# Two reads of the attention output in a fused kernel: 32-column TensorE tiles for one, split float32r products for part of the other

## The chip, the core and the metric

The kernel runs on one core of one Trainium2 chip. The metric is the device time of one execution in microseconds (us). The engines are named as in the profile: PE is TensorE's matmul side, PEld its weight loads, DVE is VectorE, ACT is ScalarE, POOL is GpSimd and SP is SyncE, which issues nearly all DMAs.

## What is computed

An attention between 2048 tokens and 128 state rows, followed by two feed-forward blocks, all in float32. Cut to what matters here:

```python
# x: (B=4, H=8, S=512, D=64)    state: (4, 8, 32, 64)
a      = softmax(x @ state^T / 8);   xread = a  @ state    # tokens read the state
a2     = softmax(state @ x^T / 8);   sread = a2 @ x        # the state reads the tokens
t = concat([xread, sread], axis=2) -> (2176 tokens, 512)   # 544 per batch
t = ((t @ w_a) * (t @ w_b)) @ w_out                        # d_ff 1536
t = softplus(t @ w_in) @ w_out2                            # d_ff 2048
```

The 128 rows of `sread` (32 states in 4 batches) go through the feed-forward blocks as tokens of their own.

## The kernel before

Every operation is written down first as a step with a cost for each engine that could do it (`Plan.add`). `Plan.go` then runs through the steps as a list scheduler: an engine that is free takes, among the steps that are ready by the costs, the one that was written first, and the order found in this way is the order of each engine's instruction queue. A step that writes a new buffer also needs a free slot in its space (`Plan.place`, line 172), and the buffers of some helpers ask that a number of slots stay free (`spare`). F is the space of 44 float32 slots, R that of 50 float32r slots (128 x 512 words each; ten of them are set aside for the last batch), and K is the eight PSUM banks. When the x of a batch is no longer needed, its four slots join R (`xr` in the trace; for the last batch F, `xf`).

Products take one of two forms. `Products.one` with float32 operands is one product, which the trace shows as two MATMUL records. `Products.three` with operands split into a high and a low float32r half is three products, one record each. `split_to` (line 500) makes the halves: a cast to float32r (`copy`, line 422, on ACT or DVE) and a subtraction (`tt`, line 430, on DVE, or on POOL where DVE has a queue). Every matmul of `one` has line 476 in the trace, every transpose line 491. `convert` (line 524) turns the loaded 64-bit weights into float32 (ACT line 415, DVE lines 438, 442 and 430).

The first feed-forward block is done in NHS = 6 parts `s` of 256 gate columns, and in each part over the four batches `b`. Part 0 also holds the attention: `scores_of`, `state_softmax`, and `sread(b)` (line 677), which takes the softmax of the state's scores and multiplies it with x. In `sread` a bank `pr[g]` holds four of the eight heads. For each of the four chunks `c` of 128 tokens and each pair of heads `j`, one product has 64 weight columns (two heads of 32 states) and 128 moving columns (the two heads' 64 columns of x). Of its 64 x 128 result only the two blocks of a head with itself are used. ACT then scales the 128 x 128 block by the softmax sums, PE turns it, and four copies of 64 x 64 put the used blocks into `srt`.

`state_w` multiplies the state with the weights of a part, `gates_of(s, b)` gives the gates of the tokens of batch `b`, `y_part` multiplies them with `w_out`. `read_x(s)` (line 792) gives the gates of the 128 `sread` tokens: four float32 products of 128 x 128 weights from `srt` with 512 columns of `ab[s, p]` (the converted `w_a` and `w_b`). For parts 0 and 1 it is written in part 1, from part 2 on right after `gates_of(s, 0)`; `read_y(s)` uses the result. The second block follows, in which `split_y` splits the result of a batch and `bring_w2` brings and splits the weights `w_in` and `w_out2`; its first three units are brought in part 5.

Of the kernel before, what the change touches and what calls it, by code (L numbers as in the profile page):

```python
# [12 lines left out]
AF = mybir.ActivationFunctionType  # L13
# [4 lines left out]
P = 128  # L18
# [99 lines left out]
def made(x):  # L118
    return x.ap() if isinstance(x, Ref) else x
# [209 lines left out]
def attention_moe_moe2(ctx, tc, x, state, w_a, w_b, w_out, w_in, w_out2, out):  # L329
# [12 lines left out]
    B, H, S, D = x.shape  # L342
# [5 lines left out]
    KD = DM // P  # L348
# [4 lines left out]
    scale = 1.0 / float(D) ** 0.5  # L353
# [21 lines left out]
    def small():  # L375

        return Buf(M, 1)

    def cols(ap):

        out = ap
        if isinstance(ap, Ref):
            b, was = ap.buf, ap.buf.at
            if was is None:
                b.at = b.space.tiles[0][0]
            if b.space in X:
                b.space.tiles[0][3].setdefault("tile", None)
            out = shaped(ap)
            b.at = was
        n = 1  # L390
        for k in out[1:]:
            n *= k
        return n
# [8 lines left out]
    def in_psum(*aps):  # L402
        return any(isinstance(a, Ref) and a.buf.space is K for a in aps)


    def act_us(n, psum=False):
        return 0.165 + (0.00086 if psum else 0.0009) * n
# [4 lines left out]
    def activation(o, i, func, **kw):  # L412
        also = [v for v in kw.values() if isinstance(v, Ref)]
        acc = [kw["accum_out"]] if "accum_out" in kw else []
        give = lambda: nc.scalar.activation(  # L415
            made(o), made(i), func, **{k: made(v) for k, v in kw.items()})
        plan.add({"act": (act_us(cols(o), in_psum(i)), give)}, [i, *also], [o, *acc])

    def copy(o, i):
        n, ps = cols(o), in_psum(i)  # L420
        ways = {
            "act": (act_us(n, ps), lambda: nc.scalar.copy(made(o), made(i))),  # L422
            "dve": (dve_us(n, ps), lambda: nc.vector.tensor_copy(made(o), made(i)),  # L423
                    *([] if ps else [True])),
        }
        plan.add(ways, [i], [o])

    def tt(o, a, b, op):
        n, ps = cols(o), in_psum(a, b)
        put = lambda eng: lambda: eng.tensor_tensor(  # L430
            out=made(o), in0=made(a), in1=made(b), op=op)
        ways = {"dve": (dve_us(n, True), put(nc.vector), *([] if ps else [True]))}
        if not ps:
            ways["pool"] = (0.23 + 0.00215 * n, put(nc.gpsimd))
        plan.add(ways, [a, b], [o])

    def ts(o, i, s1, op0):
        give = lambda: nc.vector.tensor_scalar(made(o), made(i), s1, None, op0=op0)  # L438
        plan.add({"dve": (dve_us(cols(o), False), give, True)}, [i], [o])
# [7 lines left out]
    def reduce(o, i, op):  # L447
        give = lambda: nc.vector.tensor_reduce(  # L448
            out=made(o), in_=made(i), axis=AX.X, op=op)
        plan.add({"dve": (dve_us(cols(i), True), give)}, [i], [o])  # L450

    def reciprocal(o):
        plan.add({"dve": (0.2, lambda: nc.vector.reciprocal(made(o), made(o)))}, [o], [o])  # L453
# [46 lines left out]
    def split_to(i, hi, lo):  # L500
        copy(hi, i)
        tt(lo, i, hi.bitcast(F32), ALU.subtract)

    def split(v, spare=0):

        h, l = Buf(R, v.run, spare), Buf(R, v.run, spare)
        split_to(v.all(), h.all(), l.all())
        return h, l
# [96 lines left out]
    def xn(b, p, c):  # L605

        return xs[b][p].rearrange("q (h c d) -> q c h d", h=2, d=D)[:, c]
# [10 lines left out]
    for n, i in enumerate((zs, zt)):  # L618
        ps = Buf(K, 1)
        m = Products()  # L620
# [8 lines left out]
    srt = Buf(F, 1)  # L629
# [4 lines left out]
    def quarter(b, i):  # L634

        return i ^ b % 2

    def turned(src, i=0):

        ps = Buf(K, 2)  # L640
        m = Products()
        for g in range(2):
            for c in range(4):
                m.turn(ps[g][:, c * P:c * P + P], src[i + g][:, c * P:c * P + P])
        m.end()
        return ps
# [30 lines left out]
    def sread(b):  # L677
        t = raw.pop(b)
        nm, sum2 = small(), small()
        nm_, sum_ = nm[0][:, 0:2], sum2[0][:, 0:2]  # L680
        reduce(nm_, t.all(), ALU.max)
        ts(nm_, nm_, -scale, ALU.mult)
        for g in range(2):
            activation(
                t[g], t[g], AF.Exp, bias=nm[0][:, g:g + 1], scale=scale,
                accum_out=sum2[0][:, g:g + 1],
            )
        ts(sum_, sum_, 1e-9, ALU.add)
        reciprocal(sum_)
        pa = turned(t)  # L690
        a2 = Buf(F, 2)
        copy(a2.all(), pa.all())
        pr = Buf(K, 2)
        m = Products()
        for g in range(2):
            for c in range(4):
                for j in range(2):
                    m.one(
                        pr[g][64 * j:64 * j + 64, 0:P].rearrange("p (h d) -> p h d", h=2),
                        a2[g][:, c * P + 64 * j:c * P + 64 * j + 64],  # L700
                        xn(b, 2 * g + j, c), c == 0, c == 3, us=0.23,
                    )
        m.end()

        for g in range(2):
            sd = a2[g][:, 0:P]
            activation(sd, pr[g][:, 0:P], AF.Identity, scale=sum2[0][:, g:g + 1])
            m = Products()
            m.turn(pr[g][:, P:2 * P], sd)
            m.end()  # L710
        for i in range(2):
            for g in range(2):
                src = pr[g][64 * i:64 * i + 64, P:2 * P]
                src = src.rearrange("p (j q n) -> p j q n", j=2, q=2)
                if b % 2:
                    src = src[:, :, ::-1]
                copy(
                    srT[64 * i:64 * i + 64, 2 * g:2 * g + 2, NS * b:NS * b + NS], src[:, :, i]
                )
# [39 lines left out]
    sw, ab = {}, {}  # L759
# [32 lines left out]
    def read_x(s):  # L792

        ps = Buf(K, 1)
        m = Products()
        for p in range(KD):
            m.one(ps[0], srt[0][:, p * P:p * P + P], ab[s, p][p % 2], p == 0, p == KD - 1, us=0.87)
        m.end()
        t = Buf(F, 1)
        ab_ = t[0][:, 0:HW]  # L800
        copy(ab_, ps[0][:, 0:HW])
        tt(ab_, ab_, ps[0][:, HW:W], ALU.mult)
        pt = Buf(K, 1)
        m = Products()
        for j in range(2):
            m.turn(pt[0][:, j * P:j * P + P], t[0][:, j * P:j * P + P])
        m.end()
        if s == 0 and len(Y32) == B:
            gs[s] = Buf(F, 1)
            copy(gs[s][0][:, 0:HW], pt[0][:, 0:HW])  # L810
            return
        gs[s] = Buf(R, 1)
        split_to(pt[0][:, 0:HW], gs[s][0][:, 0:HW], gs[s][0][:, HW:W])

    gs, wo, y = {}, {}, {}

    def bring_wo(s):
        w = fetch(("wo", s), 2)
# [111 lines left out]
    for s, b in steps:  # L930
# [15 lines left out]
        if s == SREAD:  # L946
            sread(b)
        if s and b == 0:
            if s > SREAD + 1:
                read_x(s)  # L950
            bring_wo(s)
        if s == SREAD + 1 and b < SREAD + 2:
            read_x(b)
# [85 lines left out]
    for q, b, k in steps:  # L1039
# [5 lines left out]
        for c0, n in cuts_of(b):  # L1045
            ps = Buf(K, 1)
            m = Products()
            for p in range(KD):
                c = p * HW + ff % 2 * P
# [47 lines left out]
```

## Time and profile before

| | before |
|---|---|
| median of 3 runs | 759.64 us (759.14 to 759.84) |
| the profiled execution | 758.87 us, span 757.1 us |
| PE busy | 733.0 us (97%), 3828 records |
| DVE busy | 583.4 us (77%), 735 instructions |
| ACT busy | 401.8 us (53%), 644 instructions |
| POOL busy | 32.7 us (4%), 19 instructions |
| granted TensorE clock | 0.998 of full speed |

Times in the views count from the start of the span. A share of busy time is a mean over stages with different limits, so the stage is read first and the share second. A group of matmuls is given with its first start and the end of its last record; the ends of matmuls are modelled, so the time that a group takes on PE is better read from its start to the start of what follows.

### The profile page before, as it was taken

The page shows a single profiled execution, that of the slowest core. Times are in us where ns is not written, and L with a number is a line of the kernel's source. Part 1 is how long each engine was busy: PE and PEld are TensorE (multiplying, and loading weights), DVE is VectorE, ACT ScalarE, POOL GpSimd, SP SyncE. Part 2 cuts the span into 40 slices and gives each one's busy share as a digit, 9 for nine tenths or more (in the row PEclk, how much of TensorE's full clock was granted, in tenths as well). Part 3 has the DMA queues.
Part 4 walks back from the last instruction along what each step waited for, and adds up shares of the span by engine and source line. Part 5 has one row for each costly group of instructions (what it writes and reads, how often), then busy time and mean ns, then how long its engine had stood idle before and what let it go on. Part 6 is the DMA issues. An engine that isn't in the chain of part 4 may idle for free.

```text
span 757.1 us, 9417 instructions
## 1 busy us (share of the span) xinstructions
PE 733.0 (97%) x3828; PEld 581.8 (77%) x3828; DVE 583.4 (77%) x735; ACT 401.8 (53%) x644; POOL 32.7 (4%) x19
## 2 busy tenths in 40 slices
PE   5889999999999999999999999999999999999996
PEld 4447677777777777778888798888988889888895
DVE  4999987768677868889999767665769888665673
ACT  4767753232323424424395586656666667656562
POOL 0000000000001000000211100100110011100000
PEclk9999999999999999999999999999999999999999
DMA  9611321103112113133111000000111100001112
GB/s 309 205 59 54 130 93 54 58 1 112 56 44 68 56 56 111 56 110 114 56 56 56 1 1 1 0 1 1 55 57 56 55 1 1 1 0 56 56 56 70
DMA packets 22351, 45.17 MB, mean 60 GB/s; under 512 B 2212, under 2 KB 6308, under 8 KB 22308
## 3 DMA queue, kind: packets, MB, share of 16 engines
q1 hardware_dynamic: 21764, 43.52, 17.0%
q10 hardware_dynamic: 544, 1.05, 0.4%
q8 instruction: 30, 0.49, 0.3%
q14 instruction: 13, 0.11, 0.0%
HBM read 40.11 MB, written 4.46 MB: 59 GB/s over the span
## 4 chain that ended last, share of the span: by engine, by line
PE 77%; DVE 19%; issue 1%; DMA 1%; ACT 1%; SPq 0%; DVEq 0%
PE PS L476 76%; DVE SF L442 6%; DVE SF L430 5%; DVE SR L430 3%; DVE SM L448 2%; DVE SF L438 2%; PE PS L491 1%; DMA x<-in_x 1%; DVE xr L430 1%; ACT SF L415 0%; SPq L459 0%; DVE SM L453 0%; ACT SR L422 0%; DVE SR L423 0%; DVE xf L430 0%
## 5 line engine op out<-in xcount | busy, mean ns | idle before, releaser
L476 PE MATMUL PS<-SR 128*128 128x512 f32 (+2 forms) x1878 | 461.0, 378 | 2.5 <-DVE SF L430 1.2
L476 PEld LDWEIGHTS PS<-SR 128*128 128x128 f32 x1878 | 340.1, 188 | 71.2 <-issue 3.6
L415 ACT ACTIVATE SF<-SF 128x512 f32<-128x512 f32 (+3 forms) x259 | 165.7, 650 | 14.1 <-DMA SF<-in_moe_w_b 7.2
L476 PE MATMUL PS<-SR,xr 128*128 128x512 f32 (+2 forms) x568 | 159.3, 384 | 0.0
L430 DVE TENSOR_TENSOR SF<-SF,PS 128x1024 f32<-128x1024 f32 (+2 forms) x100 | 97.7, 985 | 47.9 <-PE PS L476 47.4
L422 ACT CAST SR<-SF 128x1024 fp32r<-128x1024 f32 (+3 forms) x103 | 75.5, 735 | 107.5 <-DVE SF L430 107.2
L442 DVE SCALAR_TENSOR_TENSOR SF<-SF 128x512 f32<-128x512 f32 (+4 forms) x139 | 131.6, 949 | 1.1
L476 PEld LDWEIGHTS PS<-SR,xr 128*128 128x128 f32 x568 | 105.0, 188 | 24.3 <-issue 2.6
L422 ACT COPY SF<-PS 128x1024 f32<-128x1024 f32 (+3 forms) x87 | 62.3, 737 | 110.2 <-PE PS L476 103.9
L476 PE MATMUL PS<-xr,SR 128*128 128x512 f32 x378 | 120.3, 392 | 0.0
L430 DVE TENSOR_TENSOR SR<-SF,SR 128x512 fp32r<-128x512 f32 (+3 forms) x96 | 82.9, 868 | 23.4 <-ACT SR L422 23.3
L442 DVE SCALAR_TENSOR_TENSOR SF<-PS,SF 128x512 f32<-128x512 f32 (+2 forms) x77 | 46.6, 605 | 54.9 <-ACT SF L415 54.9
L476 PEld LDWEIGHTS PS<-xr,SR 128*128 128x128 f32 x378 | 70.9, 188 | 16.8 <-DVE SF L430 0.8
L430 DVE TENSOR_TENSOR SF<-SF 128x512 f32<-128x512 f32 (+3 forms) x97 | 79.7, 822 | 1.7
L476 PE MATMUL PS<-SF 64*32 64x512 f32 (+2 forms) x592 | 65.2, 551 | 1.0 <-ACT SF L422 1.0
L438 DVE TENSOR_SCALAR SF<-SF 128x1024 uint32<-128x1024 uint32 x67 | 45.9, 689 | 18.8 <-ACT SF L415 18.4
L415 ACT ACTIVATE SF<-PS 128x512 f32<-128x512 f32 (+2 forms) x76 | 39.9, 526 | 30.8 <-PE PS L476 29.8
L430 POOL TENSOR_TENSOR SF<-SF 128x1024 f32<-128x1024 f32 x9 | 24.0, 2663 | 507.4 <-DVE SF L442 386.1
L476 PEld LDWEIGHTS PS<-SF 64*32 64x32 f32 (+1 forms) x592 | 22.0, 117 | 26.8 <-issue 22.6
L422 ACT CAST xr<-SF 128x1024 fp32r<-128x1024 f32 (+3 forms) x26 | 21.3, 821 | 33.9 <-DVE SF L430 33.9
L422 ACT CAST SR<-PS 128x1024 fp32r<-128x1024 f32 (+2 forms) x24 | 20.6, 866 | 20.1 <-PE PS L491 12.1
L476 PE MATMUL PS<-xr,xr 128*128 128x512 f32 x80 | 29.0, 391 | 0.0
(56 smaller groups left out, 274.1 us busy)
## 6 DMA issues: line engine op xcount, KB each, us to landing
SF<-in_moe_w_out SPq DMA_DIRECT2D x14, 1024.0 KB, 4.9
SF<-in_moe_w_in SPq DMA_DIRECT2D x8, 1024.0 KB, 5.4
SF<-in_moe_w_a SPq DMA_DIRECT2D x11, 512.0 KB, 4.1
SF<-in_moe_w_b SPq DMA_DIRECT2D x11, 512.0 KB, 5.0
x<-in_x SPq DMA_DIRECT2D x8, 512.0 KB, 9.9
out<-SF SPq DMA_DIRECT2D x13, 256.0 KB, 2.6
out<-xf SPq DMA_DIRECT2D x4, 256.0 KB, 2.6
SF<-in_moe_w_a ACTq DMA_DIRECT2D x1, 512.0 KB, 4.2
```

The costliest lines, as they stand in the source:

```text
L415: give = lambda: nc.scalar.activation(made(o), made(i), func, **{k: made(v) for k, v in kw.items()})
L422: "act": (act_us(n, ps), lambda: nc.scalar.copy(made(o), made(i))),
L430: put = lambda eng: lambda: eng.tensor_tensor(out=made(o), in0=made(a), in1=made(b), op=op)
L438: give = lambda: nc.vector.tensor_scalar(made(o), made(i), s1, None, op0=op0)
L442: give = lambda: nc.vector.scalar_tensor_tensor(out=made(o), in0=made(a), scalar=s, in1=made(b), op0=op0, op1=op1)
L448: give = lambda: nc.vector.tensor_reduce(out=made(o), in_=made(i), axis=AX.X, op=op)
L476: self.all.append(lambda: nc.tensor.matmul(made(o), made(w), made(x), start=first, stop=last, **kw))
L491: self.all.append(lambda: nc.tensor.transpose(made(o), made(i), ident))
```

## The change

`sread` computes for each head alone: 32 weight columns (32 states) and 64 moving columns (64 columns of x), on the column tile of 32 that its place in the bank names. Only the used blocks are computed, the block that is scaled and turned has 64 columns in place of 128, and the planner's cost of a product goes from 0.23 to 0.03 us, with twice as many products. `read_x` keeps the float32 products for parts 0 and 1; from part 2 on it splits `srt` (once) and the four blocks `ab[s, 0]` to `ab[s, 3]` (as two pairs), and makes three float32r products in place of each float32 product.

```diff
             for c in range(4):
-                for j in range(2):
+                for i in range(4):
+                    q = 32 * quarter(b, i)
                     m.one(
-                        pr[g][64 * j:64 * j + 64, 0:P].rearrange("p (h d) -> p h d", h=2),
-                        a2[g][:, c * P + 64 * j:c * P + 64 * j + 64],
-                        xn(b, 2 * g + j, c), c == 0, c == 3, us=0.23,
+                        pr[g][q:q + 32, 0:D], a2[g][:, c * P + q:c * P + q + 32],
+                        xn(b, 2 * g + i // 2, c)[:, i % 2], c == 0, c == 3, us=0.03,
+                        tile_position=(0, q),
                     )
...
-            sd = a2[g][:, 0:P]
-            activation(sd, pr[g][:, 0:P], AF.Identity, scale=sum2[0][:, g:g + 1])
+            sd = a2[g][:, 0:D]
+            activation(sd, pr[g][:, 0:D], AF.Identity, scale=sum2[0][:, g:g + 1])
             m = Products()
-            m.turn(pr[g][:, P:2 * P], sd)
+            m.turn(pr[g][0:D, P:2 * P], sd)
...
-                src = pr[g][64 * i:64 * i + 64, P:2 * P]
-                src = src.rearrange("p (j q n) -> p j q n", j=2, q=2)
+                src = pr[g][0:D, P:2 * P].rearrange("p (j q n) -> p j q n", j=2, q=2)
...
     def read_x(s):
         ps = Buf(K, 1)
+        whole = s < WHOLE
+        if not whole:
+            if not srparts:
+                srparts.append(split(srt))
+            whl = split(ab[s, 0], 6) + split(ab[s, 2], 6)
         m = Products()
         for p in range(KD):
-            m.one(ps[0], srt[0][:, p * P:p * P + P], ab[s, p][p % 2], p == 0, p == KD - 1, us=0.87)
+            c = slice(p * P, p * P + P)
+            w = [ab[s, p]] if whole else whl[p // 2 * 2:p // 2 * 2 + 2]
+            m.three(ps[0], [i[0][:, c] for i in ([srt] if whole else srparts[0])],
+                    [i[p % 2] for i in w], p == 0, p == KD - 1)
...
-    gs, wo, y = {}, {}, {}
+    WHOLE = 2
+    gs, wo, y, srparts = {}, {}, {}, []
```

## Rows read from the trace of the kernel before

**Rows 1.** The page: busy us, share, instructions; then the granted PE clock by slices.

```profile
PE 733.0 (97%) x3828; PEld 581.8 (77%) x3828; DVE 583.4 (77%) x735; ACT 401.8 (53%) x644; POOL 32.7 (4%) x19
...
PEclk9999999999999999999999999999999999999999
```

**Rows 2.** Busy us by stretch (columns as in the first line).

```profile
core 0: us, PE busy (x) PEld busy (x) DVE busy (x) ACT busy (x) POOL busy (x), PEclk, DMA share, GB/s
...
40.00:60.00 20.00, 17.41 (x141) 10.56 (x140) 19.93 (x25) 14.01 (x26) 0.00 (x0) 1.00 0.32 107
60.00:80.00 20.00, 19.03 (x140) 13.90 (x138) 19.93 (x26) 15.24 (x26) 0.00 (x0) 1.00 0.16 53
...
200.00:250.00 50.00, 50.00 (x255) 37.39 (x261) 36.37 (x36) 14.96 (x17) 2.39 (x1) 1.00 0.18 63
250.00:300.00 50.00, 50.00 (x248) 37.65 (x233) 38.80 (x38) 15.84 (x18) 0.00 (x0) 1.00 0.20 64
300.00:330.00 30.00, 30.00 (x161) 21.43 (x160) 25.54 (x24) 11.74 (x12) 0.00 (x0) 1.00 0.26 88
330.00:355.00 25.00, 25.00 (x112) 20.49 (x111) 21.24 (x22) 10.31 (x12) 0.00 (x0) 1.00 0.42 136
355.00:422.00 67.00, 67.00 (x299) 55.50 (x298) 66.72 (x71) 39.22 (x60) 13.79 (x5) 1.00 0.16 52
422.00:747.00 325.00, 324.62 (x1563) 277.44 (x1562) 231.07 (x370) 205.16 (x385) 15.23 (x6) 1.00 0.07 23
```

**Rows 3.** PE in order of time: start, us, group, idle before and its releaser.

```profile
49.95 1.97 PE L476 MATMUL PS<-x,SF 128*64 128x128 f32 x32
...
53.98 1.95 PE L476 MATMUL PS<-SF 64*32 64x256 f32 x48
57.11 1.66 PE L476 MATMUL PS<-SR 128*128 128x512 f32 x6 [1.18 <-DVE SF L430]
...
62.92 1.66 PE L476 MATMUL PS<-SR 128*128 128x512 f32 x6 [0.77 <-DVE SR L430]
64.52 1.97 PE L476 MATMUL PS<-x,SF 128*64 128x128 f32 x32
...
77.97 3.01 PE L476 MATMUL PS<-SR 128*128 128x512 f32 x12 [0.16 <-ACT SF L422]
80.91 1.97 PE L476 MATMUL PS<-x,SF 128*64 128x128 f32 x32
82.81 1.65 PE L476 MATMUL PS<-SR 128*128 128x512 f32 x6
85.86 1.28 PE L491 MATMUL PS<-ident,SF 128*128 128x128 f32 x10 [1.40 <-DVE SF L430]
...
96.02 1.97 PE L476 MATMUL PS<-x,SF 128*64 128x128 f32 x32
97.92 1.66 PE L476 MATMUL PS<-SR 128*128 128x512 f32 x6
```

**Rows 4.** PE groups by shape: tile, moving operand, records; busy us, mean ns of one.

```profile
L476 PE MATMUL PS<-SF 64*32 64x512 f32 x384 | 24.9, 597 | 0.1
L476 PE MATMUL PS<-x,SF 128*64 128x128 f32 x128 | 7.9, 276 | 0.0
L476 PE MATMUL PS<-SF 64*32 64x256 f32 x128 | 5.1, 385 | 1.0 <-ACT SF L422 1.0
```

**Rows 5.** PE in order of time, the first eight records of one group alone.

```profile
53.98 0.45 PE L476 MATMUL PS<-SF 64*32 64x256 f32 x8
```

**Rows 6.** PE in order of time around `read_x(2)`, and a run of float32r products.

```profile
167.41 3.59 PE L476 MATMUL PS<-SF 128*128 128x512 f32 x8
170.44 3.31 PE L476 MATMUL PS<-SR,xr 128*128 128x512 f32 x12
173.59 0.38 PE L491 MATMUL PS<-ident,SF 128*128 128x128 f32 x2
...
347.04 5.60 PE L476 MATMUL PS<-SR 128*128 128x512 f32 x24
352.48 0.39 PE L476 MATMUL PS<-xr 128*128 128x512 f32 x1
```

**Rows 7.** Groups by shape between 100 and 430 us: the two halves of a split.

```profile
L422 ACT CAST SR<-SF 128x1024 fp32r<-128x1024 f32 x25 | 26.2, 1049 | 31.3 <-DVE SF L430 31.2
L430 DVE TENSOR_TENSOR xr<-SF,SR 128x1024 fp32r<-128x1024 f32 x5 | 6.1, 1223 | 0.0
```

**Rows 8.** PE in order of time: the wait at the end of the busy DVE stretch.

```profile
422.82 7.37 PE L476 MATMUL PS<-SR 128*128 128x512 f32 x30 [0.32 <-ACT SR L422]
```

## The prediction

> **What bounds the kernel now.** I read the page first: PE is busy 97% of the span at full clock [rows 1], so PE time looks like what is for sale. A mean hides stages, so the table of stretches came next. From 40 to 80 us DVE is busy 19.93 us of every 20, while PE is not [rows 2]. In that stage PE waits for DVE again and again: 1.18 us at 57.11, 0.77 at 62.92 and 1.40 at 85.86 [rows 3]. Up to about 86 us the bound is therefore DVE. From 100 us on PE is busy all the time, while DVE has room: it is idle 13.6 us of 200 to 250, 11.2 of 250 to 300 and 4.5 of 300 to 330 [rows 2]. From 355 to 422 both are full, DVE with 66.72 of 67 us [rows 2], and at the end of it PE waits 0.32 us for a cast that hangs on DVE [rows 8]. After that PE is the bound up to the last output, with 0.4 us idle in 325 [rows 2]. So PE time removed before 86 us should be worth nothing, after 86 us its full length, provided that DVE keeps up at 422.
>
> **The state's read on 32-column tiles.** There are four `sread` groups, at 49.95, 64.52, 80.91 and 96.02 us, each of 32 records, which are 16 products of two records [rows 3]. A group lasts 1.97 us from its first start to the end of its last record; without the last record's own 0.27 us [rows 4], 1.70 us for 32 records is far less than 32 x 0.276 = 8.8 us, so records overlap. The tile is 128 x 64 [rows 4], so two products lie side by side, 16 records deep, and one step of a tile takes about 1.70 / 15 = 0.11 us. The change makes 32 products of two records, in four tiles side by side: again 16 records deep. What becomes shorter is the step. Records with 512 and 256 moving columns differ by 597 - 385 = 212 ns, 0.83 ns a column [rows 4]; 64 columns fewer than 128 take away 53 ns. The step falls from 0.11 to about 0.056 us, and the group costs PE 16 x 0.056 = 0.90 us in place of some 1.75 us: 0.85 us less.
>
> No row shows four tiles of 128 x 32, so this has bounds on both sides. On the good side, eight records on tiles of 64 x 32 run side by side: the first eight of a group take 0.45 us in all, of which one record is 0.385, so they start (0.45 - 0.385) / 7 = 9 ns apart [rows 4, 5]. At 9 ns a record 64 records would need 0.6 us, less than the 0.90 of the columns, so the columns bind. On the bad side, if the four tiles didn't overlap at all, 64 x 0.056 = 3.6 us, 1.85 us more than now. A middle row is 48 records of 64 x 32 tiles in 1.95 us [rows 3], at most 1.95 / 48 = 41 ns each with moving operands up to eight times longer. I take 0.90 because it is nearest to both rows with small tiles, in which records do overlap; the range keeps 0.90 to 3.6.
>
> The Trainium skill (TensorE: Matmul & The Clock Gate, section "Wait — 56ns, not 53.3ns?") speaks against the step: it states that the distance from one start to the next never drops below about 25 ns, however small the product is. By that an estimate for 64 records is 1.6 us, and the gain of a group would be 0.15 in place of 0.85 us. The 9 ns above don't bear it out between different tiles [rows 4, 5].
>
> What counts of it: the first three groups lie in the DVE-bound stage. If they end earlier, PE waits longer for DVE at 57.11, 62.92, 77.97 and 85.86 [rows 3], and I cost their gain at nothing. The work that hides it is DVE's; if that cover were gone, they would bring up to 3 x 0.85 = 2.55 us. The fourth group at 96.02 lies behind the last of these waits and counts in full: -0.85 us. Scaling and turning 64 columns instead of 128 saves ACT and PE some tenths in the same places, which I leave at nothing; the four copies stay as they are. No DMA is added or moved.
>
> **The gates of these tokens as float32r.** A float32 `read_x` has 8 records. From its start at 167.41 to the transposes at 173.59 lie these 8 and 12 float32r records, 6.18 us [rows 6]. A float32r record takes (352.48 - 347.04) / 24 = 0.2267 us [rows 6], so 12 are 2.72 us, and the 8 are 6.18 - 2.72 = 3.46 us. The change puts 12 float32r records in place of these 8: 2.72 us. Saved per part 0.74 us, and with four parts (2 to 5), all of them in the stretch in which PE is the bound: -2.96 us.
>
> For it, each of the four parts gets two splits of 128 x 1024, and `srt` one of 128 x 512. A split is a cast of 1.05 us on ACT and a subtraction of 1.22 us on DVE [rows 7]. In all that is some 9 casts (about 9 us) and 10.4 us of subtractions, about 2.4 us per part on DVE. DVE is idle 11 to 14 us of each 50 us there, ACT over 30 [rows 2], and the inputs (`ab`) exist a part ahead, since `state_w` of the part has read them. So I cost the splits at nothing; the cover is DVE's idle time, and without it each part would cost up to 2.4 us. Part 5 has least of it, but still 4.5 us before 330 and 3.8 us from 330 to 355 [rows 2].
>
> At 422 PE now waits 0.32 us [rows 8] for the end of a stretch in which DVE has no idle time. If PE comes there 3.8 us earlier, DVE must too. Most of its work from 330 on is released by PE's results (the sums and splits of the outputs), which come earlier by the same amount; the weights of the second block don't. I take 0.3 us as lost, the size of the wait that is there now; the bound is the whole 3.8 us.
>
> **Sum.** -0.85 - 2.96 + 0.3 = -3.5 us against the profiled execution of 758.87 us (span 757.1 us): 755.4 us. The median of the runs lies 0.77 us above that execution, so the forecast for the median is 759.64 - 3.5 = 756.1 us, with its own range of 754.9 to 757.6.
>
> **The rivals.**
> - **DVE keeps the end at 422.** PE arrives early and waits. For it: 66.72 us busy of 67 [rows 2], and the existing wait [rows 8]. Against it: 8.3 us of idle DVE time from 300 to 355 [rows 2]. If all but 1 us of the gain is given back there: 758.6 us.
> - **The order changes in the DVE-bound stage.** The planner is told that an `sread` takes 32 x 0.03 = 0.96 us instead of 16 x 0.23 = 3.68, where the trace has 1.75. Its picture of PE becomes better by over 1 us four times, and DVE's queue may come out in an order in which PE waits less. If the first three groups then count too: 756.1 - 2.6 = 753.5 us. Against it: DVE's work there stays what it is and is already back to back [rows 2].
> - **The splits come late because slots are short** (the slower side). Two splits of `ab` need 8 slots of R and `srt` two for good. By the code the start of a part holds some 39 of the 52 (8 for the softmax of two batches, 8 of `w_out` in two parts, some 14 of `state_w`, 8 gates, 1), and each split asks for 6 spare. A split that only starts when `gates_of` has freed slots puts a cast and a subtraction, 1.05 + 1.22 = 2.27 us [rows 7], in front of `read_x` or of the halves of `state_w`, which ask for slots at the same time. PE's order is fixed, so it waits. At 2.27 us per part the four parts cost 9.1 us against 3.5 gained: 765.2 us. It decides from 3.5 / 4 = 0.9 us of waiting in each part. For it: the narrow count. Against it: inputs that exist a part ahead.
> - **The small tiles don't overlap.** Each group then costs 1.85 us more: the fourth in full, the other three 5.5 us less the waits that they fill (1.18 + 0.77 + 0.16 + 1.40 = 3.5 us [rows 3]), so 2.0 us. Together 756.1 + 0.85 + 1.85 + 2.0 = 760.8 us. If records are only kept apart so that a group costs what it does now, it is 757.0 us, inside the forecast's own range.
>
> **How the numbers follow.** About what a measurement of this kernel can tell from no change is 0.2%, 1.5 us: faster is under 758.1 us, slower over 761.2. Forecast 0.47, of which 0.46 is faster and 0.01 within 0.2%. Better order 0.15, faster. DVE at 422 0.17: 0.14 within, 0.03 faster. Late splits 0.13: 0.11 slower, 0.02 within. Tiles without overlap 0.08: 0.04 within, 0.03 slower, 0.01 faster. That gives faster 0.65, same 0.21, slower 0.14. The range from 752.8 to 760.4 us takes in the forecast, the better order, DVE at 422 and the milder forms of the last two, and leaves out under 2 in 10.
>
> **What would show it.** In the changed kernel's trace: four groups of 64 records on 128 x 32 tiles, each about 0.9 us from its start to what follows, against 3.6 us without overlap; PE's waits for DVE before 88 us longer than now by about what the first three groups save; from part 2 on 12 float32r records in 2.72 us where 8 float32 records took 3.46; DVE between 100 and 330 us busier by some 2.4 us per part, with no PE wait for line 430 or 422 in these parts; at about 419 a PE wait of at most some tenths. A PE wait of over 0.9 us in each part, or one of 3 us near 419, would make the prediction wrong, and so would a first stage that ends at another time than now.

## The result: 749.6 us, a gain of 10.0 us, nearly three times the forecast

The changed kernel takes 749.64 us (median of 4 runs, 749.54 to 749.76), the kernel before 759.65 us. The ratio is 0.9868, with an interval from 0.9856 to 0.9879. The forecast was 756.1 us, and its range ended at 752.8: the sign is right, the size is not. The profiled execution took 749.62 us, its span 747.8.

The page of the changed kernel (busy us, share, instructions), to be laid beside [rows 1]:

```profile
PE 725.4 (97%) x3972; PEld 580.3 (78%) x3972; DVE 591.7 (79%) x741; ACT 405.4 (54%) x647; POOL 56.3 (8%) x28
```

PE is busy 7.6 us less, DVE 8.3 us more, and POOL has nine instructions more. The stretches of the changed kernel, with the columns of [rows 2]:

```profile
40.00:60.00 20.00, 18.59 (x175) 10.72 (x174) 19.93 (x25) 15.56 (x28) 0.00 (x0) 1.00 0.15 54
60.00:80.00 20.00, 20.00 (x251) 15.35 (x250) 19.86 (x26) 15.83 (x26) 0.00 (x0) 1.00 0.15 54
...
40.00:100.00 60.00, 58.59 (x587) 41.60 (x586) 57.33 (x70) 45.00 (x78) 0.00 (x0) 1.00 0.21 72
...
347.00:412.00 65.00, 64.98 (x289) 53.50 (x288) 61.99 (x69) 40.59 (x61) 10.93 (x4) 1.00 0.22 74
```

This is the riddle. Between 40 and 80 us DVE is as full as before (19.93 and 19.86 of 20, against 19.93 and 19.93), yet PE has hardly any gap left: 1.41 us in 20, then none, where it had 2.59 and 0.97. The forecast had said that PE's waits there would become longer.

PE of the changed kernel in order of time (start, us, group, idle before and its releaser; last, the first float32 `read_x`):

```profile
43.19 1.09 PE L491 MATMUL PS<-ident,x 128*128 128x128 f32 x8 [1.11 <-DVE SF L430]
...
50.24 1.10 PE L476 MATMUL PS<-x,SF 128*32 128x64 f32 x64
51.27 1.98 PE L476 MATMUL PS<-SF 128*128 128x512 f32 x4
...
54.43 3.03 PE L476 MATMUL PS<-SR 128*128 128x512 f32 x12
...
61.28 2.78 PE L491 MATMUL PS<-ident,SF 128*128 128x128 f32 x24
...
65.01 1.10 PE L476 MATMUL PS<-x,SF 128*32 128x64 f32 x64
66.04 1.65 PE L476 MATMUL PS<-SR 128*128 128x512 f32 x6
...
77.67 1.10 PE L476 MATMUL PS<-x,SF 128*32 128x64 f32 x64
...
90.81 1.10 PE L476 MATMUL PS<-x,SF 128*32 128x64 f32 x64
...
101.76 3.59 PE L476 MATMUL PS<-SF 128*128 128x512 f32 x8
```

The same two marks stand in the kernel before, in its order of time on PE:

```profile
42.89 1.09 PE L491 MATMUL PS<-ident,x 128*128 128x128 f32 x8 [1.11 <-DVE SF L430]
...
74.02 1.91 PE L491 MATMUL PS<-ident,SF 128*128 128x128 f32 x16
...
109.21 3.60 PE L476 MATMUL PS<-SF 128*128 128x512 f32 x8
```

From the transposes of x to the first `read_x` is therefore 109.21 - 42.89 = 66.32 us before and 101.76 - 43.19 = 58.57 after. This stretch, called the first stage below, is 7.75 us shorter. The forecast for it was 0.85. The waits of 1.18, 0.77, 0.16 and 1.40 us [rows 3] are gone; the two waits that are left, 0.30 and 1.11 us, come before 43.19, so between the two marks PE isn't idle at all.

### The profile page after: what moved, and what is told of

The parts are those of the page before. It is cut to its first block, busy times and chain, and to the rows that moved or that the text cites. A ratio compares the mean times of both kernels' runs of the same rounds, so it can differ in the third digit from the quotient of the medians.

```text
span 747.8 us, 9721 instructions
## 1 busy us (share of the span) xinstructions
PE 725.4 (97%) x3972; PEld 580.3 (78%) x3972; DVE 591.7 (79%) x741; ACT 405.4 (54%) x647; POOL 56.3 (8%) x28
## 4 chain that ended last, share of the span: by engine, by line
PE 89%; DVE 7%; ACT 1%; DMA 1%; issue 1%; DVEq 0%; ACTq 0%
PE PS L476 88%; DVE SF L430 2%; DVE SF L442 1%; PE PS L491 1%; DVE SR L430 1%; DMA SF<-in_moe_w_b 1%; ACT SF L415 1%; DVE SM L448 1%; DVE SF L438 1%; ACT SF L422 0%; ACT xr L422 0%; DVE SR L423 0%; DVE xr L430 0%; ACT SR L422 0%; DVE SM L453 0%
## 5 line engine op out<-in xcount | busy, mean ns | idle before, releaser
L476 PE MATMUL PS<-SR 128*128 128x512 f32 (+2 forms) x1986 | 513.6, 379 | 0.0
L476 PEld LDWEIGHTS PS<-SR 128*128 128x128 f32 x1986 | 362.4, 188 | 70.7 <-issue 2.9
L476 PE MATMUL PS<-SR,xr 128*128 128x512 f32 (+2 forms) x544 | 171.7, 376 | 0.2 <-DVE SR L430 0.2
L415 ACT ACTIVATE SF<-SF 128x512 f32<-128x512 f32 (+3 forms) x246 | 152.9, 631 | 12.9 <-DMA SF<-in_moe_w_b 5.7
L430 DVE TENSOR_TENSOR SF<-SF,PS 128x1024 f32<-128x1024 f32 (+2 forms) x126 | 117.2, 942 | 38.0 <-PE PS L476 37.1
L442 DVE SCALAR_TENSOR_TENSOR SF<-SF 128x512 f32<-128x512 f32 (+4 forms) x117 | 103.1, 885 | 0.5
L476 PEld LDWEIGHTS PS<-xr,SR 128*128 128x128 f32 x338 | 63.4, 188 | 18.9 <-DVE SR L430 2.3
L476 PE MATMUL PS<-SF 64*32 64x512 f32 (+2 forms) x560 | 51.5, 549 | 1.1 <-ACT SF L422 1.0
L422 ACT CAST xr<-SF 128x1024 fp32r<-128x1024 f32 (+2 forms) x26 | 23.0, 884 | 31.8 <-DVE SF L430 31.8
L491 PE MATMUL PS<-ident,SF 128*128 128x128 f32 (+1 forms) x128 | 19.2, 284 | 10.7 <-DMA SF<-in_state 8.3
```

The source lines that it names most:

```text
L415: give = lambda: nc.scalar.activation(made(o), made(i), func, **{k: made(v) for k, v in kw.items()})
L430: put = lambda eng: lambda: eng.tensor_tensor(out=made(o), in0=made(a), in1=made(b), op=op)
L442: give = lambda: nc.vector.scalar_tensor_tensor(out=made(o), in0=made(a), scalar=s, in1=made(b), op0=op0, op1=op1)
L476: self.all.append(lambda: nc.tensor.matmul(made(o), made(w), made(x), start=first, stop=last, **kw))
L491: self.all.append(lambda: nc.tensor.transpose(made(o), made(i), ident))
```

## The experiments

The first theory is that of the prediction: up to 86 us DVE sets the pace. The second is its rival "better order": the planner's cost of the `sread` products, 3.68 us in all against 1.89 in the trace [rows 3], put steps in a wrong order, and a smaller number alone removes PE's waits. "First stage" in the table is measured as above in each profiled execution; medians and ratios are against the kernel before in the same session (759.5 to 759.7 us).

| run | median us | ratio (interval) | first stage us |
|---|---|---|---|
| before | 759.6 | | 66.32 |
| e1, old tiles, cost 0.06 | 755.26 | 0.9943 (0.9926 to 0.9960) | 62.03 |
| e5, old tiles, cost 0.11 | 755.16 | 0.9940 (0.9925 to 0.9955) | 61.53 |
| e6, cost 0.06 for batch 0 alone | 756.22 | 0.9957 (0.9942 to 0.9971) | 63.01 |
| e7, cost 0.06 for batches 1 to 3 | 757.56 | 0.9972 (0.9962 to 0.9982) | 64.15 |
| e2, new tiles, order of before | 759.49 | 1.0001 (0.9992 to 1.0010) | 65.82 |
| e3, new tiles, cost 0.03 | 751.84 | 0.9897 (0.9883 to 0.9912) | 58.56 |
| e4, split `read_x` alone | 757.04 | 0.9967 (0.9954 to 0.9980) | 66.34 |
| e8, the whole change, cost of before | 757.16 | 0.9966 (0.9956 to 0.9976) | 65.77 |
| after | 749.64 | 0.9868 (0.9856 to 0.9879) | 58.57 |

**The planner's number alone.** The kernel before with one constant changed. No product and no value changes, only the order of the queues; two steps also change their engine, a cast at 91.3 us (from ACT to DVE) and an addition at 180.9 us (from DVE to POOL).

```diff
-  xn(b, 2 * g + j, c), c == 0, c == 3, us=0.23,
+  xn(b, 2 * g + j, c), c == 0, c == 3, us=0.06,
```

> The kernel before with one number changed: the planner is told that an old sread product (64 weight columns, 128 moving columns) costs 0.06 us in place of 0.23, so 0.96 us per sread as in the changed kernel. No product changes; only the order of the queues may. Theory 'DVE bound' (the recorded prediction): the work and its bound are as before, 759.6 us within 1.5. Theory 'order': the planner's false 3.68 us made DVE and PE take up other work too early in part 0, and the better order alone brings most of what the first stage gained, about 5 us: 753 to 756 us. Theory 'PE time': the products' own time was the bound, no gain, 759.6 us.

It gained 4.3 us. PE is idle 60 - 58.60 = 1.40 us between 40 and 100, against 4.95 before. The two kernels in this stretch, before first:

```profile
40.00:100.00 60.00, 55.05 (x425) 38.81 (x425) 57.80 (x70) 41.54 (x71) 0.00 (x0) 1.00 0.26 88
```

and e1:

```profile
40.00:100.00 60.00, 58.60 (x443) 41.96 (x442) 55.94 (x67) 41.98 (x73) 0.00 (x0) 1.00 0.21 71
```

PE's idle time is shorter by 3.55 us, of the 4.29 us by which the stage is. So the order was worth 4.3 us by itself, with the same products and nearly the same work in total (DVE is busy 584.0 us in all, before 583.4). The theory that the stage lasts as long as it does because DVE has that much to do for it falls here.

What the order changed is seen when the stage is measured from mark to mark, before first, then e1:

```profile
42.89:109.21 66.32, 62.77 (x457) 45.53 (x458) 61.53 (x73) 45.47 (x77) 0.00 (x0) 1.00 0.24 82
```

```profile
43.30:105.33 62.03, 62.03 (x456) 45.50 (x457) 54.56 (x66) 43.66 (x74) 0.00 (x0) 1.00 0.20 69
```

PE's work is the same but for 0.7 us, and in e1 PE isn't idle between the marks. DVE does 7.0 us less before the first `read_x`. By DVE's rows the stage holds 30 instructions of weight conversions before (30.0 us) and 22 in e1 (22.0 us): eight of them now run behind the mark, where DVE has room.

**The small tiles in the old order.** The changed `sread`, with costs chosen so that the planner sees the same sums as before, also for the scaling on ACT (128 columns), and with `read_x` as before; its queues come out in the order of the kernel before.

```diff
-  xn(b, 2 * g + i // 2, c)[:, i % 2], c == 0, c == 3, us=0.03,
+  xn(b, 2 * g + i // 2, c)[:, i % 2], c == 0, c == 3, us=0.0 if i % 2 else 0.23,
...
-            activation(sd, pr[g][:, 0:D], AF.Identity, scale=sum2[0][:, g:g + 1])
+            src, by = pr[g][:, 0:D], sum2[0][:, g:g + 1]
+            plan.add({"act": (act_us(P, True), lambda sd=sd, src=src, by=by: nc.scalar.activation(
+                made(sd), made(src), AF.Identity, scale=made(by)))}, [src, by], [sd])
```

> The kernel before with the 32-column tiles in sread, but with the planner's costs of the old products and of the old 128-column scaling, so that the order of every queue is that of the kernel before; read_x is the old one. Theory 'DVE bound': only the fourth sread counts, 759.6 - 0.85 = 758.8 us. Theory 'order': the same, 758 to 759.3 us. Theory 'PE time': the PE time of the first three counts too, 3.4 us or more, 756.2 us or less.

No gain: 759.49 us. PE in order of time shows where the saved time went:

```profile
58.11 1.65 PE L476 MATMUL PS<-SR 128*128 128x512 f32 x6 [1.38 <-DVE SF L430]
...
69.04 0.50 PE L491 MATMUL PS<-ident,SF 128*64 128x128 f32 x2 [0.84 <-ACT SF L709]
...
86.86 1.28 PE L491 MATMUL PS<-ident,SF 128*128 128x128 f32 x10 [2.27 <-DVE SF L430]
```

and the stretch in one row:

```profile
40.00:100.00 60.00, 52.41 (x554) 35.18 (x553) 57.75 (x70) 41.59 (x70) 0.00 (x0) 1.00 0.26 89
```

The wait of 1.18 us has become 1.38, that of 1.40 has become 2.27, and one of 0.84 for ACT's scaling has come in. PE is idle 7.59 us in place of 4.95, which is 2.64 more, against 3 x 0.86 = 2.58 us that the first three groups became shorter: the tiles' saving is there, and in this order it is handed back as waiting. That is what the prediction had said of the first three groups; it was wrong only in taking the order as given. (The fourth group's 0.85 us, which was to count in full, doesn't show in the median, whose interval is 0.7 us wide on either side. In the trace 0.53 us of it is left: from the start of this group to the first `read_x` it is 109.70 - 97.04 = 12.66 us, before 109.21 - 96.02 = 13.19.)

**The small tiles in the new order.** The changed kernel with the old `read_x`; `sread` and its cost of 0.03 stay. Its order on DVE is that of e1.

```diff
-        whole = s < WHOLE
-        if not whole:
...
-            whl = split(ab[s, 0], 6) + split(ab[s, 2], 6)
...
-            m.three(ps[0], [i[0][:, c] for i in ([srt] if whole else srparts[0])],
+            m.one(ps[0], srt[0][:, p * P:p * P + P], ab[s, p][p % 2], p == 0, p == KD - 1, us=0.87)
```

> The changed sread with its new cost and the old read_x: the order of the queues is the same as in the run with the cost alone, only the products differ. Theory 'DVE bound': 758.8 us. Theory 'order': the first read_x of part 1 began 7.4 us earlier in the changed kernel, and all of that comes from sread, so 752 to 753 us, with about 2 to 3.4 us of difference to the run with the cost alone (in a good order PE has no waits in which saved time could be lost). Theory 'PE time': 752 to 756 us, the same as the tiles in the old order.

751.84 us, 3.42 us faster than e1, which is 4 x 0.855: here each of the four groups counts with the price that the prediction had worked out. With two orders and two kinds of tiles the table is full: tiles alone 0.1 us, order alone 4.3, both 7.75 (interval of the ratio 0.9883 to 0.9912). The whole is more than the sum of the parts.

**The split `read_x` alone.** The kernel before with the new `read_x`.

```diff
+    WHOLE = 2
...
-            m.one(ps[0], srt[0][:, p * P:p * P + P], ab[s, p][p % 2], p == 0, p == KD - 1, us=0.87)
+            m.three(ps[0], [i[0][:, c] for i in ([srt] if whole else srparts[0])],
+                    [i[p % 2] for i in w], p == 0, p == KD - 1)
```

> The old sread with its old cost, and read_x with float32r products from part 2 on. All theories: 4 x 0.74 us less PE time in the stage where PE is the bound, 756.7 us, if the splits are hidden. If splits or the changed order cost what is gained: 759 to 761 us. The changed kernel's own trace has PE waits of 0.9 us between 250 and 322 us, so up to 1 us may be lost: 757.7 us.

757.04 us, -2.55 from the 759.59 of its session; the forecast for this part was -2.96 + 0.3 = -2.66. The only wait on PE from 100 to 430 us is one of 0.44 us, in the third part:

```profile
156.51 1.09 PE L476 MATMUL PS<-SF 64*32 64x512 f32 x16 [0.44 <-DVE SF L430]
```

**The true cost.** The kernel before with a product at what the trace shows, 1.75 / 16 = 0.11 us.

```diff
-  xn(b, 2 * g + j, c), c == 0, c == 3, us=0.23,
+  xn(b, 2 * g + j, c), c == 0, c == 3, us=0.11,
```

> The kernel before with the planner told what the trace shows: 0.11 us per old sread product, 1.76 us per sread, in place of 3.68. No product changes. Theory 'order' in the form that the planner's false cost is what puts steps that aren't ready at the head of PE's queue: the same as with 0.06, about 755.3 us, PE idle from 40 to 100 us near 1.4 us. Rival 'luck of one order': any other cost gives another order with another time; anywhere from 754 to 760 us.

755.16 us, within the intervals equal to e1. The low number of the change isn't special: the measured price was enough to find a better order. It isn't the order of e1: 25 of the 30 conversion instructions stay in the stage, in place of 22, and PE again isn't idle between the marks. Each engine has as many instructions here as in the kernel before.

**Which of the costs.** The low cost for batch 0 alone (e6, shown), and for the other three alone (e7, with the two numbers changed about).

```diff
-  xn(b, 2 * g + j, c), c == 0, c == 3, us=0.23,
+  xn(b, 2 * g + j, c), c == 0, c == 3, us=0.06 if b == 0 else 0.23,
```

> The kernel before with the cost 0.06 for the first of the four sreads alone (batch 0), 0.23 for the other three. PE waits after the first sread (1.18 us at 57.11 and 0.77 at 62.92 in the kernel before) should go if they come from the planner's picture of this sread, the later ones (0.16 and 1.40 us) stay: 759.6 - 1.95 = 757.6 us. If one decision early on carries the whole order, all is gained: 755.3 us. If it depends on the later ones: 759.6 us.

> The complement: the cost 0.06 for the sreads of batches 1, 2 and 3, and 0.23 for the first. The first two waits stay, the two later ones go: 759.6 - 1.56 = 758.0 us. If the first decision carries all: 759.6 us; if the later ones do: 755.3 us.

-3.4 and -2.1 us, where the sums of the single waits had said -2.0 and -1.6: both matter, and they overlap, since they make 5.5 together and 4.3 in one kernel (e1). The first `sread` carries most of it. What its cost does is seen in DVE's queue. DVE of the kernel before, in order of time:

```profile
54.50 1.21 DVE L448 TENSOR_REDUCE SM<-SF 128x32 f32<-128x1024 f32 x1
55.63 0.30 DVE L438 TENSOR_SCALAR SM<-SM 128x2 f32<-128x2 f32 x2
55.84 1.22 DVE L430 TENSOR_TENSOR SF<-SF,PS 128x1024 f32<-128x1024 f32 x1
...
69.17 0.68 DVE L438 TENSOR_SCALAR SF<-SF 128x1024 uint32<-128x1024 uint32 x1
...
72.45 2.35 DVE L442 SCALAR_TENSOR_TENSOR SF<-SF 128x1024 uint32<-128x1024 uint32 x2
74.72 1.21 DVE L430 TENSOR_TENSOR SF<-SF,PS 128x1024 f32<-128x1024 f32 x1
75.85 1.21 DVE L448 TENSOR_REDUCE SM<-PS 128x32 f32<-128x1024 f32 x1
```

DVE of the changed kernel:

```profile
54.80 1.22 DVE L430 TENSOR_TENSOR SF<-SF,PS 128x1024 f32<-128x1024 f32 x1
55.94 1.22 DVE L448 TENSOR_REDUCE SM<-SF 128x32 f32<-128x1024 f32 x1
...
65.93 1.22 DVE L448 TENSOR_REDUCE SM<-PS 128x32 f32<-128x1024 f32 x1
...
81.74 2.35 DVE L442 SCALAR_TENSOR_TENSOR SF<-SF 128x1024 uint32<-128x1024 uint32 x2
```

The planner believed that the first `sread` keeps PE for 3.68 us, so that the result of the products behind it would be ready late, and put a reduction (line 448) ahead of the multiplication of line 430 that reads it. In the trace PE, whose queue is in order too, stood 1.18 us at 57.11 until this multiplication was done [rows 3]. In the changed kernel the two have changed places (54.80 and 55.94). PE's own queue has another order there as well, and its 12 float32r products start at 54.43 with no wait. Twenty microseconds later it is the same on a larger scale: before, DVE converts weights of the next part (lines 438 and 442, 69.17 to 74.7 us) ahead of the last batch's softmax, whose reduction comes at 75.85; after, that reduction comes at 65.93 and a like conversion at 81.74. So DVE was full, but in part with work that nobody waited for yet. The queues of PE and ACT change with DVE's in all of these runs; none changes DVE's order alone, so how much of the 4.3 us comes from conversions that left the stage and how much from changed places within it isn't shown.

**The whole change with the old cost.** The changed kernel, 32 products at 0.115 us, 3.68 us together.

```diff
-  xn(b, 2 * g + i // 2, c)[:, i % 2], c == 0, c == 3, us=0.03,
+  xn(b, 2 * g + i // 2, c)[:, i % 2], c == 0, c == 3, us=0.115,
```

> The whole change with one number undone: the planner is told 0.115 us per 32-column product, 3.68 us per sread as before. Theory 'order': the tiles bring nothing in the old order (0.1 us measured), the float32r products what they bring alone (2.55 us): 757.0 us. Theory 'the tiles' own time': 749.6 us plus at most 1 us.

757.16 us. One number in the planner decides over 7.5 of the 10.0 us; what is left is the split `read_x`.

**More work for DVE.** How near is DVE to being the bound in each order? The two instructions of lines 438 and 442 are issued twice in three weight conversions, which alters no value, with the planner's costs and so the order unchanged; e9 is on the kernel before, e10 on the changed one. The expectations took 0.60 + 1.13 us for each, 5.2 in all. In the rows of e9 and e10 the second issue costs 0.72 + 1.27 us by the distances of the starts, 6.0 us in all.

```diff
+        for s in plan.steps[first:] if twice else ():
+            cost, give, *more = s.ways["dve"]
+            s.ways = {"dve": (cost, lambda give=give: (give(), give()), *more)}
...
+    TWICE = (("wo", 0), ("ab", 1, 0), ("ab", 1, 2))
```

> The kernel before with two DVE instructions of three weight conversions (w_out of part 0, the two halves of w_a and w_b of part 1) issued twice; the second time writes the same values. That is 3 x (1.13 + 0.60) = 5.2 us more DVE work between 58 and 75 us, in the same order of every queue. Theory 'in the old order DVE is what PE waits for': nearly all of it is paid, 759.6 + 4 to 5 = 763.6 to 764.8 us. Theory 'DVE is only filled with early work and has slack': under 1 us, 760.6 us at most.

> The changed kernel with the same six extra DVE instructions (5.2 us of DVE work), which lie between 60 and 86 us there. PE does not wait for DVE between 44 and 250 us in this order. Theory 'in the new order DVE, though as busy, is not the bound': most is hidden, under 2 us, 751.6 us at most. Theory 'DVE bounds the stage in any order': all is paid, 754.8 us.

e9 lost 6.1 us against the 759.48 of its session (765.56, ratio 1.0079, 1.0064 to 1.0094): about as much as the extra work, as a DVE on the path has to. e10 lost 5.4 us against the changed kernel (755.04; ratio to before 0.9942, 0.9927 to 0.9957). The expectation of under 2 us for it fell. The starts of the `sread` groups show where the time was lost. In e10, on PE:

```profile
42.80 1.06 PE L491 MATMUL PS<-ident,SF 128*128 128x128 f32 x8 [1.27 <-DVE SF L430]
44.98 1.55 PE L491 MATMUL PS<-ident,x 128*128 128x128 f32 x8 [1.11 <-DVE SF L430]
46.32 4.87 PE L476 MATMUL PS<-SF 128*128 128x512 f32 x8
...
53.72 1.10 PE L476 MATMUL PS<-x,SF 128*32 128x64 f32 x64
...
68.67 1.10 PE L476 MATMUL PS<-x,SF 128*32 128x64 f32 x64
...
82.59 1.10 PE L476 MATMUL PS<-x,SF 128*32 128x64 f32 x64
...
95.77 1.10 PE L476 MATMUL PS<-x,SF 128*32 128x64 f32 x64
```

Against 50.24, 65.01, 77.67 and 90.81 these are late by 3.48, 3.66, 4.92 and 4.96 us. In e9 the four groups start at 52.86, 69.95, 87.09 and 102.22, late by 2.91, 5.43, 6.18 and 6.20 [rows 3]. The extra work lay in other places than the expectations thought, near 30, 49 and 66 us. The first piece, 2.0 us before 43 us, delayed both kernels: there DVE is on the path in either order. Not all of the first delay is DVE's, though. In e10 the transposes at 44.98 are late by 1.79 us; the other 1.69 us of the 3.48 come between there and 51.03, where PE's granted clock was low (last section). In e9 it is 0.73 of the 2.91 us. Of the second and third pieces, 2 x 2.0 = 4.0 us, the old order paid 6.20 - 2.91 = 3.3 and the new one 4.96 - 3.48 = 1.5. So the new order has about 2.5 us of room on DVE from 49 to 90 us, not the comfort that the first theory for e10 had given it; in the changed kernel's first stage DVE is busy 55.87 of 58.57 us. In the new order PE and DVE are nearly balanced.

**Moving the border of `read_x`.** The changed kernel with the split from part 1 on (e11, shown), and from part 3 on (e12, `WHOLE = 3`).

```diff
-    WHOLE = 2
+    WHOLE = 1
```

> The changed kernel with read_x split from part 1 on (one float32 read_x left). One more read_x of 3.46 us becomes 2.72 us: 749.6 - 0.74 = 748.9 us if its splits are hidden; DVE is idle only 10 us from 100 to 150 there, and two splits more come with one of srt, so 749 to 751 us if they are not.

> The changed kernel with read_x split from part 3 on, so three split reads in place of four: 749.6 + 0.74 = 750.4 us by PE's time alone; 749.4 us if the PE wait of 0.4 to 0.5 us that the changed kernel has at 250 to 322 us goes with it.

Both come out slower than the change as it is, and than both of their expectations: 752.23 us (ratio 0.9905, 0.9889 to 0.9922) and 751.12 (0.9889, 0.9875 to 0.9904). In e12 one float32 `read_x` more costs 1.5 us by the medians, where the prediction's price is 0.74. The interval of e12 overlaps that of the change, and the spans of the two profiled executions differ by 748.7 - 747.8 = 0.9 us, near the price; the rest isn't shown to be more than noise. The two PE waits of the changed kernel (0.4 and 0.5 us, below) are still there. In e11 the splits come earlier and reach into the first stage:

```profile
40.00:100.00 60.00, 56.50 (x572) 38.76 (x571) 56.83 (x67) 45.30 (x79) 4.79 (x2) 1.00 0.26 89
```

PE is idle 3.50 us there, against 1.41. New are waits for casts of ACT (line 422), 1.8 us in all, and DVE isn't busier than after. The first stage is 105.05 - 43.27 = 61.78 us, 3.2 more than after, and what follows it is 1.0 us shorter.

## Why the prediction was wrong

**The first stage is the step that failed.** "I cost their gain at nothing. The work that hides it is DVE's": this rested on DVE's 19.93 us of 20 [rows 2]. In the old order it is true (e2), but the change also alters the order, and the prediction had this as a rival with a chance of 0.15, and argued against it that "DVE's work there stays what it is and is already back to back". In total the work did stay; but e1 shows that another order, with 22 in place of 30 conversion instructions before the first `read_x`, is 4.3 us faster. A full engine with a queue in order is the bound only if everything in its queue is needed by then. The conversions at 69.17 to 74.7 us were not: in the changed kernel like ones come after 80 us, and PE waits for none of them. A first stage that ends at another time than before was one of the signs by which the prediction said it would be wrong.

The chain of waits shows the same from the end. In the stretch of 40 to 110 us it had been, in the kernel before, by line:

```profile
by line: PE PS L476 31.4%; DVE SF L430 18.4%; DVE SR L430 11.4%; DVE SM L448 11.3%; DVE SF L442 10.8%; DVE SF L438 5.5%; PE PS L491 3.4%; DVE xr L430 3.2%; issue 3.2%; DVE SM L438 1.3%; DVE SM L453 1.3%
```

and in the changed kernel it is PE alone from 43.19 us on:

```profile
by line: PE PS L476 83.6%; PE PS L491 12.1%; DVE SF L430 3.4%; DVE SR L430 1.6%; issue 0.1%
```

Of the first, 16.3% are lines 442 and 438, which stand mostly for conversions of weights. A chain that runs through an engine back to back for some 46 us, with work in it that serves a later stage, is a question about the order and not yet a bound. The Trainium skill (Perfetto Trace Analysis, section "Identifying the Most-Contended Engine") would name the engine with the highest occupancy here, which between 40 and 80 us is DVE, and work on that first; the traces don't bear it out for an in-order queue, since e1 gained 4.3 us with DVE busy 584.0 us in all in place of 583.4.

**The rival was there and was mis-sized.** "753.5 us" counted the PE time of three more groups, 2.55 us. It left out that a better order removes PE's own waits as well, 1.18 + 0.77 + 0.16 + 1.40 = 3.5 us [rows 3]; with them it would have said 750.0, against 749.64 measured. The prediction had used these same 3.5 us in another rival, and so had them at hand. That 750.0 is so near is in part luck: for the first stage these terms give 0.85 + 2.55 + 3.5 = 6.9 us, and it became 7.75 shorter; for the rest the prediction had 2.66, and it became 1.85.

**The price of the tiles was right.** Forecast 0.85 us for a group; from its start to what follows it was 51.84 - 49.95 = 1.89 us before and 51.27 - 50.24 = 1.03 after, 0.86 less, and e3 against e1 gives 0.855. The group itself was put at 0.90 in place of 1.75 us; both were too low, by 0.13 and 0.14 us, so the difference came out. That the price of the fourth group counts in full held in the new order; in the old one 0.53 us of it is left (e2).

**`read_x` was right.** Forecast -2.66 us, measured -2.55 alone (e4) and 751.84 - 749.64 = -2.20 behind the new `sread`. The splits are hidden but for single waits: 0.44 us in e4, and in the changed kernel two, of 0.44 and 0.52 us, which PE's waits for DVE between 100 and 430 us list:

```profile
PE PS L476 <- DVE SR L430: 0.5, 1, 0.5
PE PS L491 <- DVE SF L430: 0.4, 1, 0.4
```

In size that is one tenth of the rival "late splits", 9.1 us; that short slots cause them isn't shown. One thing the prediction didn't see: it put all subtractions on DVE, but POOL took part of them. Between e3, which has the old `read_x`, and the change POOL's busy time goes from 35.1 to 56.3 us, and that of DVE only from 583.6 to 591.7.

**No loss at 422.** PE is idle 0.02 us from 347 to 412, the stretch that answers to 355 to 422; even the 0.32 us of [rows 8] are gone, and DVE has 3 us of room there. The 0.3 that I took as lost was not.

**The sum by the runs.** The first stage became 7.75 us shorter. From the first `read_x` to the end of the span it is 757.1 - 109.21 = 647.89 us before and 747.8 - 101.76 = 646.04 after, 1.85 shorter. The stage begins 0.30 us later. Together that is -9.30, the difference of the two spans. Of the 1.85 us the prediction's terms with the waits as found make -2.96 + 0.96 - 0.32 = -2.3; the 0.5 us between the two, and the 0.77 us by which the profiled execution of before lay below its median, stay open.

## What to carry to other kernels

Before an engine's 99% in a stage is called the bound, look at what is in its queue: if part of it serves a later stage, the order may be what binds, and a change of a planner's cost alone can show it in one run. The costs of a hand-made planner should be taken from the trace: one number that was twice too large cost 4.3 us by itself and would have hidden 7.5 us of this change. A saving on an engine that waits should be tried in both orders, since in one of them it can be worth nothing and in the other its full length.

## What the runs showed of the hardware that wasn't expected

**Four column tiles side by side.** The first four records of a group of the changed kernel, on PE in order of time, and the group's form (busy us, mean ns of one):

```profile
50.24 0.26 PE L476 MATMUL PS<-x,SF 128*32 128x64 f32 x4
```

```profile
L476 PE MATMUL PS<-x,SF 128*32 128x64 f32 x256 | 4.4, 220 | 0.0
```

The 64 records end after 1.10 us, of which the last one is 0.22: (1.10 - 0.22) / 63 = 14 ns from one start to the next. The Trainium skill (TensorE: Matmul & The Clock Gate, section "Wait — 56ns, not 53.3ns?") gives a floor of about 25 ns; between records of different tiles the trace doesn't agree.

**The clock after short waits.** In e10 the 8 float32 records at 46.32 us took 4.87 us, where the same records of the changed kernel took 3.60. Its row for that stretch:

```profile
44.00:48.00 4.00, 3.02 (x10) 2.02 (x11) 4.00 (x6) 3.79 (x6) 0.00 (x0) 0.68 0.00 0
```

The granted clock is 0.68, a mix of the two levels of 1.2 and 2.4 GHz. Ahead of it PE had waited 1.27 us at 42.80 and 1.11 at 44.98, with transposes between. With waits of 0.30 and 1.11 us in the same places the changed kernel kept 1.00. The slow transposes and products together took 1.69 us of e10's first delay of 3.48, about half of it.

The length of the waits alone doesn't decide it. In e2 PE waited 0.44 us at 55.64 and 1.38 at 58.11, and the 6 float32r records behind took 1.65 us. In e8, with the same waits in the same places, they took a microsecond more:

```profile
58.14 2.65 PE L476 MATMUL PS<-SR 128*128 128x512 f32 x6 [1.38 <-DVE SF L430]
```

There the granted clock was 0.62 from 58 to 60 us. What made the difference these runs don't show.
